# Decode attention with an MLP on one core: the first head's keys in two transfers

## The chip, the cores and the metric

The kernel runs on one core of a Trainium2 chip. A core has TensorE (matrix products, with a separate path that loads the stationary operand), VectorE, ScalarE, GpSimd, and SyncE, which here issues nearly all transfers. Sixteen DMA engines move data between the chip's memory (HBM) and the core's on-chip memory (SBUF); TensorE writes its results to accumulators (PSUM). Engines run side by side and order themselves with semaphores.

The metric is the time of one execution on the device, in microseconds. Lower is better.

## What is computed

One new token passes through an attention block with a key and value cache and then through a small MLP, each behind a layer norm and with a residual. There are 32 heads of width 128, a cache of 32768 positions, bf16 data, and a model width of 512.

```python
def _A_ref(x, k_cache, v_cache, wq, wo):
    q = (x @ wq).reshape(B, Sq, H, Dh).transpose(0, 2, 1, 3)
    scores = einsum("bhqd,bhkd->bhqk", q, k_cache) * (Dh ** -0.5)
    p = softmax(scores)
    o = einsum("bhqk,bhkd->bhqd", p, v_cache)
    return o.transpose(0, 2, 1, 3).reshape(B, Sq, H * Dh) @ wo

h = x + _A_ref(_layernorm(x), A_k_cache, A_v_cache, A_wq, A_wo)
h2 = h + _B_ref(_layernorm(h), B_w1, B_b1, B_w2)      # act = h * tanh(softplus(h))
```

K and V of one head are 8 MB each, so the caches together are 537 MB, nearly all that the kernel reads.

## The kernel before

**Tiles.** A head's K lies in SBUF as 128 partitions by 256 tiles of 128 columns (`SCOLS` = 256); the 256 tiles form two halves of `TPS` = 128. A ring of six slots holds half a K or V each: K of the even heads has slots 0 and 1, K of the odd heads slots 2 and 3, and V, for all heads, slots 4 and 5. WQ lies in slot 4 at first, WO later in a K slot.

**One head on TensorE and VectorE.** `head(i)` runs `keys(i, 0)` and `keys(i, 1)`, each 16 groups (`GPS`) of `GT` = 8 tiles. In `k_group`, TensorE transposes 8 tiles into one of four PSUM tiles (L663), VectorE copies them to `ering` (L668), and up to three groups later (`KEEP`) `scores` multiplies them with the head's query into `S_ps` (L641). `soft_max`, `soft_a`, `soft_b` and `soft_exp` then find the maximum over the partitions and form the exponentials in `pbuf`. `rest(i)` does for the head before: `soft_c` (the sum), `pv` (256 products with the tiles of V, L689) and `oev`. `turn` runs once, after head 0: it is head 0's `soft_a`, `soft_b` and `soft_exp`.

**Order.** TensorE's and VectorE's program is a loop over heads: head(0), turn, then head(i), rest(i) for the others, and at the end `mid` (the product of 31 heads with WO), the last rest, and `tail` (the rest of the projection and the MLP). On TensorE the loop body stands once and is run 32 times; the waits in it compare a semaphore with a value that is computed from the round's counter (`_loop_waits`). The addresses of the 8 key tiles of a group are also computed from the counter (`key_addresses`, L520): for each group but a head's first, that happens right after the transposes of the group before it, ahead of the scores that follow there.

**Transfers.** SyncE (SP) works through the list `order`: WQ, K0, K1, V0, K2, V1, K3, V2, and so on to WO, V31 and the MLP's weights (issues at L532). Each issue waits for what frees its place (`freed_by`): K of head h for the release of both halves of K of head h-2, V for the product of the head before with its V, and V0 for WQ's release after the projection of the query. WQ itself is issued ahead of the program's blocks (L840). A K or V is one transfer of 8 MB, other than V of the last head, which comes in six pieces after `CUTS["v"]`. For such pieces there are semaphores of their own, `cut_sems`; the heads whose V comes whole still have waits on them in the loop's body, so SP adds the missing counts once, as listed by `uncut`.

**Waits on keys.** A head's first transpose waits for "keys_in", the count of the slot pair that holds its K. Nothing waits within a head for keys.

Of the kernel before, what the change touches and what calls it, by code (L numbers as in the profile page):

```python
# [291 lines left out]
def bass_sequential_preLN__mha_block_cached__dense_activation_mish__decode_kernel(  # L292
    nc: bass.Bass,
    A_x: bass.AP,
    A_k_cache: bass.AP,
    A_v_cache: bass.AP,
    A_wq: bass.AP,
    A_wo: bass.AP,
    B_x: bass.AP,
    B_w1: bass.AP,  # L300
    B_b1: bass.AP,
    B_w2: bass.AP,
    out: bass.AP,
):
    build_kernel(nc, A_x, A_k_cache, A_v_cache, A_wq, A_wo, B_w1, B_b1, B_w2, out)


def build_kernel(nc, A_x, A_k_cache, A_v_cache, A_wq, A_wo, B_w1, B_b1, B_w2, out):
# [3 lines left out]
    H = HD // Dh  # L312
# [9 lines left out]
    TPS = 128  # L322
    SLOT = TPS * Dh
    HALVES = Sk // (128 * TPS)
    SCOLS = HALVES * TPS
    GT = 8
# [95 lines left out]

    CUTS = {"k": [], "v": [TPS // 2, TPS, 192, 224, 240]}

    def pieces(what):
        kind, h = what
        at = CUTS["v"] if what == ("v", H - 1) else []
        return list(zip([0] + at, at + [SCOLS]))  # L430

    def cut_at(kind, h, r):
        return r in [r0 for r0, _ in pieces((kind, h))]

    def uncut(what):


        kind, h = what
        for r in CUTS[kind]:
            if not cut_at(kind, h, r) and (h == 0 or cut_at(kind, h - 1, r)):  # L440
                n = 1
                while h + n < H and not cut_at(kind, h + n, r):
                    n += 1
                yield r, n
# [4 lines left out]
    order += [WO, ("v", H - 1), WL] + W1P + W2P  # L449
    cut_sems = {k: {r: sem(f"cut_{k}_{r}") for r in CUTS[k]} for k in CUTS}  # L450

# [9 lines left out]
    def slot_of(what):  # L461
        if what in HOMES:
            return HOMES[what]
        if what[0] in ("w1", "w2"):
            return HOMES[WL]
        return V_HOME if what[0] == "v" else what[1] % 2 * HALVES
# [6 lines left out]
    def ready_wait(what):  # L473
        if what == WL:
            return (s_wl, 16)
        return (ready[slot_of(what)], 16 * fills[what])

    def free_name(what):
        return "free" + "_".join(map(str, what))

    def freed_by(what):
        if what == WO:
            return done_with("k", H - 2, 0, SCOLS)
        if what[0] == "k" and what[1] > 1:
            return done_with("k", what[1] - 2, 0, SCOLS)
        if what == ("v", 0):
            return [free_name(WQ)]
        return []

    def tiles_of(what):  # L490
        return ring[:, slot_of(what):slot_of(what) + HALVES, :].rearrange("p s (r d) -> p (s r) d", d=Dh)

    def keys_of(cache, h):
        return cache[0, h, :, :].rearrange("(p r) d -> p r d", r=SCOLS)
# [8 lines left out]
    def done_with(kind, h, r0, r1):  # L503
        if kind == "v":
            return [f"pv{h}_{r1}" if r1 in V_EVENTS else f"pv{h}"]
        return [free_name(("k", h, half)) for half in range(HALVES) if r0 < (half + 1) * TPS and r1 > half * TPS]
# [1 line left out]
    events = {}  # L508

    def key_tile(S, at):  # L510
        if at == 0:
            key_addresses(S, 0)
        off = S.home + at * Dh * 2
        return ring8[:, bass.ds(off, Dh * 2)].bitcast(BF16)

    def key_addresses(S, at):

        if S.emit and S.only == PE and S.counter is not None:
            for r in range(at, at + GT):
                nc.tensor.lower_val(S.home + (r * Dh * 2 + ring_at + 2 * (Dh - 1)))  # L520

    def program(S):
# [3 lines left out]
        v = nc.vector  # L526
# [4 lines left out]
        def start(dst, src, s):  # L531
            S.dma(SP, lambda: sp.dma_start(dst, src).then_inc(s, 16))  # L532
# [3 lines left out]
        for what in order:  # L536
            slot = slot_of(what)
            if what == ("k", 1):
                S.stay(SP)
            S.wait(SP, freed_by(what))  # L540
            flat = ring[:, slot, :]
            if what[0] == "wq":
                S.wait(SP, ["b1z"])
                start(b1r[0:FJ, :], B_b1[0:FJ * 128].rearrange("(j p) -> j p", j=FJ), s_b1)
                start(b1r[FJ:FJ + 1, 0:FLAST], B_b1[FJ * 128:F].rearrange("(o p) -> o p", o=1), s_b1)
            elif what[0] == "wo":
                start(flat, A_wo.rearrange("(p j) n -> p (j n)", j=32), ready[slot])
            elif what == WL:
                start(wol_v, A_wo[(H - 1) * Dh:H * Dh, :], s_wl)
            elif what[0] == "w1":  # L550
                k = what[1]
                start(w1_v[:, k, :], B_w1[k * 128:(k + 1) * 128, :], w1_sems[k])
            elif what[0] == "w2":
                n = what[1]
                if n + 1 < len(W2_J):
                    j0, j1 = W2_J[n], W2_J[n + 1]
                    start(w2_v[:, j0:j1, :], B_w2[j0 * 128:j1 * 128, :].rearrange("(j p) n -> p j n", p=128), w2_sems[n])
                else:
                    start(w2_v[0:FLAST, FJ, :], B_w2[FJ * 128:F, :], w2_sems[n])
            else:  # L560
                kind, h = what
                rows = keys_of(A_k_cache if kind == "k" else A_v_cache, h)
                for r0, r1 in pieces(what):
                    if kind == "v" and h:
                        S.wait(SP, done_with(kind, h - 1, r0, r1))
                    start(tiles_of(what)[:, r0:r1, :], rows[:, r0:r1, :], cut_sems[kind][r0] if r0 else ready[slot])
                for r, n in uncut(what):
                    S.dma(SP, lambda r=r, n=n: sp.sem_inc(cut_sems[kind][r], 16 * n))
        S.dma(SP, lambda: sp.dma_start(out[0, 0, :].rearrange("(c m) -> c m", c=KC), outr[0:128:32, :]).then_inc(s_out, 16),
              waits=["fin"])  # L570
# [46 lines left out]
        for h in range(H):  # L617
            for kc in range(KC):
# [4 lines left out]
                       waits=(["xn0", ready_wait(("wq",))] if h == 0 and kc == 0 else ()))  # L623
# [20 lines left out]
        def flush(keep):  # L644
            while len(pend) > keep:
                scores(*pend.pop(0))

        def k_group(h, half, gi):
            what = ("k", h)
            bg = count[0]  # L650
            count[0] += 1
            tb = T_b[bg % NT]
            for r in range(GT):
                at = half * TPS + gi * GT + r
                waits = []
                if r == 0:
                    if at == 0:
                        waits.append("keys_in")
                    waits.append("identb")
                names = []  # L660
                if r == GT - 1:
                    names = [f"trb{bg}"] + ([free_name(what + (half,))] if gi == GPS - 1 else [])
                S.step(PE, lambda r=r, at=at: t_.matmul(tb[:, r * 128:(r + 1) * 128], key_tile(S, at), identb[:, :],  # L663
                                                        is_transpose=True, start=True, stop=True),
                       name=(names or None), waits=waits, kind=f"tr{bg % (2 * GPS)}")
            if half * TPS + (gi + 1) * GT < SCOLS:
                key_addresses(S, half * TPS + (gi + 1) * GT)
            S.step(DVE, lambda: v.tensor_copy(ering[:, bg % NE, :, :].rearrange("p r d -> p (r d)"), tb[:, :]),  # L668
                   name=f"ev{bg}", waits=[f"trb{bg}"],
                   kind=f"ev{bg % (2 * GPS)}")  # L670
            pend.append((h, half * TPS + gi * GT, bg))
            flush(KEEP)


        def pv(h, r0, r1):
            what = ("v", h)
            vt = tiles_of(what)
            for r in range(r0, r1):
                waits = []
                if r == 0:  # L680
                    waits += [f"exp{h}", ready_wait(what)]
                if r in CUTS["v"]:
                    waits.append((cut_sems["v"][r], 16 * (h + 1)))
# [43 lines left out]
        def keys(h, half):  # L727
            for gi in range(GPS):
                k_group(h, half, gi)
# [107 lines left out]
    log = {}  # L837
    counted = _Sched(nc, False, events, sems, log)
    program(counted)
    nc.sync.dma_start(ring[:, slot_of(WQ), :], A_wq.rearrange("(p k) n -> p (k n)", k=KC)).then_inc(ready[slot_of(WQ)], 16)  # L840
    with nc.Block() as block:
        for eng_name, attr in ((POOL, "gpsimd"), (SP, "sync"), (DVE, "vector"), (ACT, "scalar"), (PE, "tensor")):
            emitter = _Sched(nc, True, events, sems, log, only=eng_name)

            def _run(eng, emitter=emitter):
                program(emitter)
            getattr(block, attr)(_run)
            assert emitter.cnt == counted.cnt
# [31 lines left out]
```

## Time and profile before

| | us |
|---|---|
| median of 3 runs | 1288.19 (1287.94 to 1292.16) |
| profiled execution, its own time | 1288.21 |
| its span in the profile | 1286.4 |
| TensorE busy (products / loads) | 1017.4 / 989.9 |
| VectorE busy | 715.6 |
| ScalarE busy | 20.7 |

The mean granted clock of TensorE was 0.769 of full speed.

How to read it: the page gives, for one execution, the busy time of each engine, then the span in 40 slices with the busy tenths of each engine, the granted clock, the busy share of the 16 DMA engines and the GB/s. The chain of waits is followed back from the last instruction, at each step to what released it; its pieces give start, length and what ran. "issue" is time in which an engine waited for nothing that the profile shows. In the timeline a row gives the start, the length, the engine, the line and the operands, and in brackets the idle time before it with what ended it. In the view by windows a share of the DMA engines above 1 in a short window comes from packets that are counted where they begin.

### The profile page before, as it was taken

Reading aid. Unit: us, or ns where it says so; the run is one execution under the profiler, and the core shown is the slowest. Engines: PE = TensorE matmul, PEld = TensorE weight load, DVE = VectorE, ACT = ScalarE, POOL = GpSimd, SP = SyncE. Lnnn points to the kernel's source line nnn. Section 1 sums busy time; section 2 is a strip of 40 time slices with the busy share of each in tenths; the row PEclk is TensorE's granted clock in tenths of the full one; section 3 lists DMA queues with packets and bytes.
Section 4 is the critical chain, followed back from the end, with each engine's and each line's share of the span. In section 5 each row is a group of like instructions: output and inputs, shape, how many; then the busy total and the mean of one; then the engine's idle time right before and its main releaser. Section 6 shows DMA issues by size and latency. Waiting matters only on the chain.

```text
span 1286.4 us, 54403 instructions
## 1 busy us (share of the span) xinstructions
PE 1017.4 (79%) x25044; PEld 989.9 (77%) x25044; DVE 715.6 (56%) x1252; ACT 20.7 (2%) x71; POOL 0.8 (0%) x8
## 2 busy tenths in 40 slices
PE   1789777897777887777887777887777987777987
PEld 1789777887777887777887777887777887777985
DVE  0676444666545666544666454666445666444661
ACT  0000000000000000000000000000000000000000
POOL 0000000000000000000000000000000000000000
PEclk9888677887767887777887677887767887777885
DMA  9978999999999999999999999999999999999998
GB/s 422 419 336 359 424 424 454 426 424 452 428 424 434 446 424 424 454 426 424 450 430 424 424 456 424 424 454 426 424 442 438 424 424 454 426 424 452 428 423 354
DMA packets 12440, 548.35 MB, mean 426 GB/s; under 512 B 1327, under 2 KB 2832, under 8 KB 3600
## 3 DMA queue, kind: packets, MB, share of 16 engines
q1 hardware_dynamic: 12430, 548.22, 98.8%
q8 instruction: 8, 0.13, 0.0%
q10 hardware_dynamic: 2, 0.00, 0.0%
HBM read 548.21 MB, written 0.00 MB: 426 GB/s over the span
## 4 chain that ended last, share of the span: by engine, by line
DMA 55%; DVE 23%; PE 18%; SPq 2%; issue 1%; POOL 0%; POOLq 0%
DMA ring<-in_A_k_cache_dram 55%; DVE ering L668 23%; PE ops L689 9%; PE tps L663 7%; SPq L532 2%; PE sps L641 1%; PE hlp L713 1%; PE hlp L708 1%; DMA ring<-in_B_w_dram 1%; PE hlp L723 0%; PE tps L825 0%; DVE pmax L702 0%; DVE outr L830 0%; DVE gmax L710 0%; SPq L68 0%
## 5 line engine op out<-in xcount | busy, mean ns | idle before, releaser
L663 PE MATMUL tps<-identb,ring 128*128 128x128 bf16 x8192 | 668.7, 232 | 232.7 <-DMA ring<-in_A_k_cache_dram 227.3
L668 DVE COPY ering<-tps 128x1024 bf16<-128x1024 bf16 x1024 | 669.1, 692 | 283.4 <-PE tps L663 282.6
L663 PEld LDWEIGHTS tps<-identb,ring 128*128 x8192 | 522.5, 104 | 235.4 <-issue 235.4
L641 PE MATMUL sps<-qcur,ering 128*128 128x1 bf16 x8192 | 343.8, 164 | 7.7 <-DVE ering L668 6.6
L641 PEld LDWEIGHTS sps<-qcur,ering 128*128 128x128 bf16 x8192 | 309.3, 97 | 10.6 <-DVE ering L668 9.4
L689 PEld LDWEIGHTS ops<-pbuf,ring 128*128 128x128 bf16 x8192 | 226.6, 103 | 15.6 <-issue 12.3
L689 PE MATMUL ops<-pbuf,ring 128*128 128x1 bf16 x8192 | 231.2, 165 | 2.4 <-DMA ring<-in_A_v_cache_dram 2.4
L697 DVE TENSOR_TENSOR oT<-ops,rtotc 128x1 f32 x31 | 5.0, 161 | 107.1 <-PE ops L689 107.1
L710 DVE TENSOR_REDUCE gmax<-hlp 1x1 f32<-1x128 f32 x32 | 8.9, 279 | 63.1 <-PE hlp L708 63.1
L715 DVE TENSOR_SCALAR nbias<-hlp 128x1 f32<-128x1 f32 x32 | 5.1, 159 | 63.5 <-PE hlp L713 63.5
L718 ACT ACTIVATE pbuf<-sps,nbias 128x256 bf16<-128x256 f32 x32 | 15.2, 474 | 1236.4 <-PE ops L689 1171.5
L702 DVE TENSOR_REDUCE pmax<-sps 128x1 f32<-128x256 f32 x32 | 13.6, 425 | 14.3 <-PE sps L641 14.3
L708 PE MATMUL hlp<-ident,pmax 128*1 128x128 f32 x64 | 17.7, 375 | 2.4 <-issue 2.4
L713 PE MATMUL hlp<-gmax,onesmat 1*128 1x1 f32 x64 | 18.5, 356 | 0.4 <-DVE gmax L710 0.4
L713 PEld LDWEIGHTS hlp<-gmax,onesmat 1*128 1x128 f32 x64 | 15.8, 304 | 1.3 <-DVE gmax L710 0.9
L723 PE MATMUL hlp<-esum,onesmat 128*128 128x1 f32 x64 | 12.3, 261 | 5.0 <-issue 1.8
L723 PEld LDWEIGHTS hlp<-esum,onesmat 128*128 128x128 f32 x64 | 9.8, 192 | 7.6 <-issue 7.6
L620 PE MATMUL hlp<-xnT,ring 128*128 128x1 bf16 x128 | 3.5, 165 | 9.1 <-DMA ring<-in_A_wq_dram 9.1
L620 PEld LDWEIGHTS hlp<-xnT,ring 128*128 128x128 bf16 x128 | 3.5, 104 | 9.2 <-issue 9.2
L725 DVE RECIPROCAL rtotc<-hlp 128x1 f32<-128x1 f32 x32 | 5.4, 168 | 3.9 <-PE hlp L723 2.4
L624 DVE CAST qT<-hlp 128x32 bf16<-128x32 f32 x1 | 0.2, 192 | 11.3 <-PE hlp L620 11.3
L718 ACT ACTIVATION_READ_ACCUMULATOR pbuf<-sps,nbias 128x1 f32 x32 | 6.1, 192 | 0.0
(75 smaller groups left out, 37.8 us busy)
## 6 DMA issues: line engine op xcount, KB each, us to landing
ring<-in_A_v_cache_dram SPq DMA_DIRECT2D x3, 2048.0 KB, 11.2
ring<-in_A_wq_dram SPq DMA_DIRECT2D x1, 4096.0 KB, 12.1
ring<-in_A_wo_dram SPq DMA_DIRECT2D x1, 4096.0 KB, 35.2
ring<-in_B_w_dram SPq DMA_DIRECT2D x4, 344.0 KB, 16.6
ring<-in_A_v_cache_dram SPq DMA_DIRECT2D x1, 1024.0 KB, 14.2
ring<-in_A_v_cache_dram SPq DMA_DIRECT2D x2, 512.0 KB, 15.4
ring<-in_B_w_dram SPq DMA_DIRECT2D x1, 640.0 KB, 16.3
ring<-in_A_k_cache_dram SPq DMA_DIRECT2D x32, 45.1
```

The lines of the kernel that those rows point to most:

```text
L532: S.dma(SP, lambda: sp.dma_start(dst, src).then_inc(s, 16))
L620: S.step(PE, lambda h=h, kc=kc: t_.matmul(Q_REG[:, h:h + 1], wq_v[:, kc, h * Dh:(h + 1) * Dh], xnT[:, 0, kc:kc + 1], start=(kc == 0), stop ...
L641: S.step(PE, lambda r=r: t_.matmul(S_ps[:, col0 + r:col0 + r + 1], ering[:, bg % NE, r, :], qcur[:, :], start=True, stop=True), name=(name ...
L663: S.step(PE, lambda r=r, at=at: t_.matmul(tb[:, r * 128:(r + 1) * 128], key_tile(S, at), identb[:, :], is_transpose=True, start=True, stop ...
L668: S.step(DVE, lambda: v.tensor_copy(ering[:, bg % NE, :, :].rearrange("p r d -> p (r d)"), tb[:, :]), name=f"ev{bg}", waits=[f"trb{bg}"], ...
L689: S.step(PE, lambda r=r: t_.matmul(o_ps[:, 0:1], vt[:, r, :], pbuf[:, r:r + 1], start=(r == 0), stop=(r == SCOLS - 1)), name=(names or Non ...
L702: S.step(DVE, lambda: v.tensor_reduce(pmax[:, :], S_ps[:, 0:SCOLS], AXX, ALU.max), name=f"pmax{h}", waits=[f"qkh{h}"], kind="pmax")
L708: S.step(PE, lambda: t_.matmul(A_REG, pmax[:, :], ident[:, :], start=True, stop=True), name=f"A{h}", waits=[f"pmax{h}", "ident", f"rcp{h - ...
L710: S.step(DVE, lambda: v.tensor_reduce(gmax[:, :], A_REG, AXX, ALU.max), name=f"gmax{h}", waits=[f"A{h}"], kind="gmax")
L713: S.step(PE, lambda: t_.matmul(B_REG, onesm[0:1, :], gmax[:, :], start=True, stop=True), name=f"B{h}", waits=[f"gmax{h}", "consts0"], kind ...
L718: S.step(ACT, lambda: a.activation(pbuf[:, :], S_ps[:, 0:SCOLS], ACTF.Exp, bias=nb[:, :], scale=SC, accum_out=esum[:, :]), name=f"exp{h}", ...
L723: S.step(PE, lambda: t_.matmul(C_REG, onesm[:, :], esum[:, :], start=True, stop=True), name=f"C{h}", waits=[f"exp{h}"], kind="C")
```

## The change

Three things change.

- K of head 0 is issued as two transfers, tiles 0 to 127 and tiles 128 to 255. The first counts on the slot's semaphore as before, the second on a new one, `cut_sems["k"][128]`.
- In the loop body, the transpose of tile 128 (group 16, the first of the second half) has a wait of its own on that semaphore, for 16 more with each head. The addresses of group 16 are no longer computed behind the transposes of group 15, ahead of the scores there, but behind these scores, just before the transposes of group 16. With the wait comes one register instruction on TensorE for the value it waits for. The body is one instruction longer.
- For the 31 heads whose K still comes whole, SP adds 16 x 31 to the new semaphore, once, right after the issue of K2.

```diff
-    CUTS = {"k": [], "v": [TPS // 2, TPS, 192, 224, 240]}
+    CUTS = {"k": [TPS], "v": [TPS // 2, TPS, 192, 224, 240]}
 
     def pieces(what):
         kind, h = what
-        at = CUTS["v"] if what == ("v", H - 1) else []
+        at = CUTS[kind] if what in (("k", 0), ("v", H - 1)) else []
         return list(zip([0] + at, at + [SCOLS]))
...
     def key_tile(S, at):
-        if at == 0:
-            key_addresses(S, 0)
+        if at in [0] + CUTS["k"]:
+            key_addresses(S, at)
...
-                for r, n in uncut(what):
+
+                for r, n in uncut(what) if kind == "v" else [(r, H - 1) for r in CUTS["k"] if h == 2]:
                     S.dma(SP, lambda r=r, n=n: sp.sem_inc(cut_sems[kind][r], 16 * n))
...
                     waits.append("identb")
+                if at in CUTS["k"]:
+                    waits.append((cut_sems["k"][at], 16 * (h + 1)))
...
-            if half * TPS + (gi + 1) * GT < SCOLS:
-                key_addresses(S, half * TPS + (gi + 1) * GT)
+            after = half * TPS + (gi + 1) * GT
+            if after < SCOLS and after not in CUTS["k"]:
+                key_addresses(S, after)
```

## The prediction

> **What bounds the kernel now.** I read the page first, for the engine that is busy throughout and for the stretches where it is not.
>
> ```profile
> span 1286.4 us, 54403 instructions
> ...
> DMA  9978999999999999999999999999999999999998
> GB/s 422 419 336 359 424 424 454 426 424 452 428 424 434 446 424 424 454 426 424 450 430 424 424 456 424 424 454 426 424 442 438 424 424 454 426 424 452 428 423 354
> ...
> q1 hardware_dynamic: 12430, 548.22, 98.8%
> q8 instruction: 8, 0.13, 0.0%
> ...
> DMA 55%; DVE 23%; PE 18%; SPq 2%; issue 1%; POOL 0%; POOLq 0%
> ```
>
> The transfers fill 98.8% of the span. So the kernel is bound by its 548 MB, except where the queue runs dry: slices 3 and 4 (64 to 129 us) move 336 and 359 GB/s where later ones move 424 or more. The view by windows confirms it (columns: window and length, busy time and count of each engine, granted clock, DMA share, GB/s).
>
> ```profile
> 64.00:104.00 40.00, 34.98 (x829) 33.50 (x827) 24.17 (x45) 1.13 (x4) 0.00 (x0) 0.76 0.70 296
> 90.00:91.00 1.00, 1.00 (x31) 1.00 (x29) 1.00 (x3) 0.00 (x0) 0.00 (x0) 1.00 0.00 0
> 178.00:1183.00 1005.00, 809.65 (x20124) 791.37 (x20124) 575.57 (x988) 14.70 (x52) 0.00 (x0) 0.76 1.00 434
> ```
>
> From 64 to 104 us the engines are busy 0.70 of the time; afterwards the share is 1.00. Why, is seen in the chain of waits (start, length, what) and in the timeline of the first 180 us (SPq rows are issues).
>
> ```profile
> 1.96 31.54 DMA ring<-in_A_k_cache_dram
> 44.61 1.54 issue
> 48.90 0.88 PE tps L663 x8
> 49.97 0.53 PE tps L663 x8
> 50.67 0.47 PE tps L663 x8
> 51.32 0.47 PE tps L663 x8
> 52.52 1.06 issue
> 58.64 2.12 issue
> 66.07 1.96 issue
> 69.56 0.80 issue
> 70.37 3.60 PE tps L663 x32
> 73.99 18.82 DVE ering L668 x29
> 93.75 1.66 PE ops L689 x64
> 98.23 3.52 PE ops L689 x128
> 102.21 40.68 DMA ring<-in_A_k_cache_dram
> 142.89 0.33 issue
> 175.60 45.07 DMA ring<-in_A_k_cache_dram
> 1181.35 45.65 DMA ring<-in_A_k_cache_dram
> 1276.03 7.41 DMA ring<-in_B_w_dram
> ```
>
> ```profile
> 12.98 3.55 PE L620 MATMUL hlp<-xnT,ring 128*128 128x1 bf16 x128 [9.10 <-DMA ring<-in_A_wq_dram]
> 16.56 0.33 SPq L532 DMA_DIRECT2D ring<-in_A_v_cache_dram  x1
> 33.91 2.31 PE L663 MATMUL tps<-identb,ring 128*128 128x128 bf16 x20 [17.38 <-DMA ring<-in_A_k_cache_dram]
> 64.53 0.33 SPq L532 DMA_DIRECT2D ring<-in_A_k_cache_dram  x1
> 101.77 0.33 SPq L532 DMA_DIRECT2D ring<-in_A_v_cache_dram  x1
> 134.49 0.33 SPq L532 DMA_DIRECT2D ring<-in_A_v_cache_dram  x1
> ```
>
> Between the key issues at 175.60 and 1181.35 lie 26 heads, 1005.75 / 26 = 38.68 us each, so one 8 MB half of a head (K or V) takes 19.34 us. K0 lands at 1.96 + 31.54 = 33.50; K1, V0 and K2 follow without a break and end at 33.50 + 3 x 19.34 = 91.5. The next transfer, V1, shares its slots with V0 and waits until head 0's product with V is over, 98.23 + 3.52 = 101.75. K3 lands at 102.21 + 40.68 = 142.89; less two transfers, 104.2. The queue therefore loses 104.2 - 91.5 = 12.7 us here, and what puts V1 so late is a pure compute chain that starts when K0 has landed: head 0 (33.91), its softmax, head 1 (70.37), the product (93.75 to 101.75). TensorE idled 17.38 us ahead of it.
>
> Later there is no such loss: a K issued at 175.60 lands after 45.07 us, though it and the V ahead of it need 38.68, so V was issued some 6.4 us before the queue ran dry.
>
> **The change, part by part.** *K0 in two pieces.* WQ has landed by 12.98 and the whole K0 was usable at 33.91, 20.93 us for 8 MB, 1.59 us more than 19.34. No row says in which half the 1.59 falls. If in the second, the first half is usable at 12.98 + 9.67 = 22.65; if in the first, at 12.98 + 20.93 - 9.67 = 24.24. I take 24.0, near the late end, which promises less. TensorE is ready long before, 12.98 + 3.55 = 16.5. Head 0 starts 33.91 - 24.0 = 9.9 us sooner.
>
> The extra issue on SP is 0.33 us at about 2 us, behind WQ's 12 us of transfer; the issues behind it (K1, then V0 after the wait for WQ's release at 16.56) find a queue with work until 33 us. Cost nothing; uncovered, 0.33.
>
> *The second half's wait, head 0.* The 17th group, the first of the second half, starts at 48.90 now, 15.0 us after the first. Shifted, it wants its keys at 39.0, and they land at about 33.5, as the whole does now. TensorE does not stop; cover, 5.5 us.
>
> *Does the rest of head 0 shift rigidly?* It holds three stalls of "issue" (1.54, 1.06, 2.12) and slow groups: from 48.90 to 49.97 a group takes 1.07 us, from 50.67 to 51.32 0.65. The same instructions in the same order, again after an idle of many us, so I take the same length. Bounds, from the first transpose to the release of the keys (33.91 to K2's issue at 64.53, 30.6 us now): with all 32 groups at 1.07 and the 4.7 us of stalls 38.9, 8.3 lost; with the 22.4 us that head 1 takes from 70.37 to 73.99 + 18.82 = 92.81, 8.2 won. Between them I allow a stretch like that of head 1's start, 12 slow groups more, 12 x 0.42 = 5.0 us lost, and the ceiling of 12.7 on the other side.
>
> *The wait in TensorE's loop, the register addition for its value, and the two address computations that now follow it.* One instruction more per head, 32 in all, and behind it stand the transposes of group 16 and all that follows. No row has this wait. The nearest is 142.89: 0.33 us from a key's landing to the first transpose, which contains a wait and two such address computations. So 0 to 0.33 per head; no gain is possible, since nothing is taken out. In heads 0 and 1, on the chain, I charge 0.15 each, 0.3 in all, as VectorE paces the groups there (29 in 18.82 us, 0.65 each) and has several tiles to work on. For the later heads the view of waits has a row (us in total, times, longest):
>
> ```profile
> PE tps L663 <- DMA ring<-in_A_k_cache_dram: 227.3, 30, 17.4
> ```
>
> Without the first, 17.4, that is 209.9 / 29 = 7.2 us a head in which TensorE stands idle for keys, so 0.33 is hidden; uncovered it would be 30 x 0.33 = 9.9 us.
>
> *SP's count for the whole heads.* It stands behind the K2 issue, which waits for head 0's release: 64.53 now, about 55 then. Head 1 wants it for its 17th group, which VectorE copies at 73.99 + 13 x 0.65 = 82.4 now; TensorE runs up to three groups ahead, so 80 now and 70 then. 15 us of cover. What queues behind it on SP is V1, not wanted there before 92.
>
> *What is late next.* With V1 issued at 101.77 - 9.6 = 92.2, the queue still runs dry for 12.7 - 9.6 = 3.1 us, so the gain is the whole shift. K1 (52.8), V0 (72.2) and K2 (91.5) have all landed before their users at 60.8, 84.2 and 92.2 (70.37, 93.75 and 101.75, each less 9.6). From V1 on every issue and landing moves with it: V2's issue (134.49, 8.4 us before K3's end at 142.89) moves too, and the end, at 1276.03 + 7.41 a landing of the last weights, is transfer-bound as before.
>
> The sum: 9.9 - 0.3 = 9.6 us. The profiled execution took 1288.21 us (span 1286.4 and 1.81 around it), the median of the runs 1288.19. 1288.21 - 9.6 = 1278.6.
>
> [...]
>
> **The rivals.** *No gain: the transfers set the time, and the earlier start ends in another wait.* For it: 98.8%, and 55% of the chain is DMA. It needs a wait between K0 and V1's issue that does not move. Each landing above comes before its user, the tightest K2 by 0.7 us. Against it, too: the 12.7 us are idle time of the very resource that binds. Time 1288.2. Chance 0.04.
>
> *The change does not do what it says: the first half isn't usable sooner.* If the engines serve both halves of K0 side by side, the first lands with the second at about 33.5, and TensorE starts at 33.9. For it: both are queued within a microsecond. Against it: WQ was queued just ahead of K0 and landed by 12.98, with K0 20.9 us later, so pieces come in order. Time 1288.5, with the 0.3 of the waits. Chance 0.03.
>
> *Slower: the longer loop body is fetched anew in every round.* Place: TensorE's loop, one instruction longer. Now the queue for instructions moves 8 packets in the whole span, so the loop is loaded once; the stalls of the first pass (1.54, 1.06, 2.12, 1.96, 0.80, together 7.48 us) show what loading costs. If the body no longer fitted, each round would lose 7.48, and from 6.4 us on it decides, as V is then issued after the queue has run dry: 1.1 us a head, 30 heads, 33 us, less 9.6 gained: 1288.2 + 23 = 1312. Against it: one instruction among over a thousand. Chance 0.04, and 0.02 for others on that side.
>
> [...] The trace's 8 packets in 32 rounds show that it is not refetched now.
>
> *More than forecast: head 0 runs shorter too and the hole closes.* 12.7 us, 1275.5; inside the range.
>
> **How the numbers follow.** Forecast and its variants 0.87, no gain 0.04, not sooner 0.03, slower 0.06. What a measurement of this kernel can tell from no change is about 0.3%, 3.9 us. The range runs from the closed hole, 1275.5, to 5.0 us lost on slow groups, 1278.6 + 5.0 = 1283.6; past it lie the rivals and the longest head 0 (8.3 lost, 1286.9), together under 0.2. The last leaves too little to be told, so of the 0.87 I give 0.02 to no change: faster 0.85, same 0.09, slower 0.06.
>
> **What would show each step.** Right: the first transposes at 23 to 24.3 us; no idle of TensorE on keys at the middle of head 0; K2's issue near 55 and V1's near 92; the share of the queue from 64 to 104 us near 0.9; keys every 38.7 us after that; 8 packets of instructions. Wrong: the first transpose at 34 (not sooner), V1 at 102 (the chain did not move), a wait before the 17th group from head 1 on (the count is late), or stalls of "issue" in later rounds, with more instruction packets.

## The result, and the profile after

The changed kernel takes 1281.96 us (median of 5 runs, 1281.40 to 1282.46); the kernel before takes 1288.65 us (median of 5, 1287.94 to 1292.16). The ratio is 0.9942, with a 95% interval of 0.9928 to 0.9957: faster by 0.58%, 6.7 us where 9.6 were forecast. The change does what it says and the gain comes from where it was expected; 2.9 us of it are missing, and the experiments are about these.

The page after, in the lines shown of before:

```profile
span 1279.6 us, 54437 instructions
...
DMA  9979999999999999999999999999999999999998
GB/s 425 420 339 426 445 440 426 426 426 459 426 426 426 449 436 426 426 426 459 426 426 426 453 432 426 426 434 451 426 426 426 457 428 426 426 436 449 426 426 355
...
q1 hardware_dynamic: 12574, 548.22, 99.3%
q8 instruction: 8, 0.13, 0.0%
```

The fourth slice moves 426 GB/s where it moved 359; the third, 339, is as poor as before. Instructions are 34 more (32 register instructions, one transfer, one count), and their queue still moves 8 packets: the loop is not fetched anew. The same windows:

```profile
64.00:104.00 40.00, 38.12 (x903) 37.33 (x901) 28.05 (x47) 0.57 (x2) 0.00 (x0) 0.80 0.83 350
90.00:91.00 1.00, 1.00 (x24) 0.97 (x21) 0.00 (x0) 0.00 (x0) 0.00 (x0) 0.50 0.00 0
178.00:1183.00 1005.00, 811.23 (x20114) 793.94 (x20112) 575.16 (x988) 14.73 (x52) 0.00 (x0) 0.76 1.00 433
```

The share of the DMA engines from 64 to 104 us rose from 0.70 to 0.83, not to the 0.9 expected: the hole is smaller and not closed. In the bulk nothing changed (1.00, 433 GB/s). The timeline after, first transposes and issues of K2, V1 and V2:

```profile
24.30 3.59 PE L666 MATMUL tps<-identb,ring 128*128 128x128 bf16 x32 [7.75 <-DMA ring<-in_A_k_cache_dram]
...
56.28 0.33 SPq L532 DMA_DIRECT2D ring<-in_A_k_cache_dram  x1
...
95.31 0.33 SPq L532 DMA_DIRECT2D ring<-in_A_v_cache_dram  x1
...
127.90 0.33 SPq L532 DMA_DIRECT2D ring<-in_A_v_cache_dram  x1
```

Against the rows of before: the first transpose is 33.91 - 24.30 = 9.6 us sooner, K2's issue 64.53 - 56.28 = 8.3, V1's 101.77 - 95.31 = 6.5, V2's 134.49 - 127.90 = 6.6. The start is right within 0.3; what was gained there is lost between the first transpose and V1's issue. The chain of waits after shows where:

```profile
34.57 2.25 issue
...
41.86 4.62 issue
46.47 0.27 PE sps L642 x4
46.74 0.88 PE tps L666 x8
47.62 0.19 PE sps L642 x8
47.81 0.88 PE tps L666 x8
...
57.80 3.06 issue
...
62.39 0.79 issue
63.19 3.55 PE tps L666 x32
...
91.51 0.59 issue
92.10 3.19 PE ops L693 x114
...
95.75 40.67 DMA ring<-in_A_k_cache_dram
```

Before, there were 1.54 + 1.06 + 2.12 + 1.96 + 0.80 = 7.48 us of "issue" up to V1's issue; now 2.25 + 4.62 + 3.06 + 0.79 + 0.59 = 11.31. That is 3.8 us more, all in the first pass through the loop. The 0.80 and 0.79 among them stand ahead of head 1's first transposes and don't belong to the first pass alone: ahead of head 2's, too, there is such a gap, of 0.88 us before and 0.87 after. The row of before:

```profile
102.61 3.59 PE L663 MATMUL tps<-identb,ring 128*128 128x128 bf16 x32 [0.88 <-issue]
```

Without them the stalls of the first pass are 6.68 us before and 10.52 after. Each sum is that of one profiled execution.

The packet records of the trace say what these waits are. The queue for instructions has one packet of 16 KB at each of these times (us from the span's start), and its eighth near the end, at 1284.8 before and 1277.9 after:

```
before  19.5  43.8  51.2  58.3  65.5  72.7  94.7
after   19.5  34.3  43.9  51.1  58.2  65.4  89.6
```

TensorE's long stalls end 2.3 to 2.6 us after such a packet has begun (after: 36.82, 46.47, 60.85, 92.10). In all kernels measured the stalls of head 0 fall at the same places of the program, behind the 4th transpose of the 14th group, behind 4 scores that follow the 21st group's transposes, and behind the 5th transpose of the 29th group, though not each kernel has all three. In the trace of before 694, 950 and 1206 instructions of TensorE lie ahead of these places, 256 from one to the next; in that of after 694 and 950 lie ahead of the first two. From this I read the stalls so: the loop is fetched block by block while TensorE runs through it for the first time, 256 instructions in a packet of 16 KB, and TensorE stands when the next block is late. The packets of the middle stand 7.1 to 9.6 us apart, where a block without stalls or slow groups takes 4.9 us (from 29.5 on the chain of after does a group every 0.65 us; a group has 34 instructions, 16 loads, 16 products and 2 for addresses, so 256 are 7.5 groups).

### The profile page after: what moved, and what is told of

Same layout as the page of the kernel before. It is cut to its first block, busy times and chain, and to the rows that moved or that the text cites. A ratio compares the mean times of both kernels' runs of the same rounds, so it can differ in the third digit from the quotient of the medians.

```text
span 1279.6 us, 54437 instructions
## 1 busy us (share of the span) xinstructions
PE 1019.0 (80%) x25044; PEld 992.2 (78%) x25044; DVE 716.1 (56%) x1252; ACT 20.8 (2%) x71; POOL 0.8 (0%) x8
## 4 chain that ended last, share of the span: by engine, by line
DMA 55%; DVE 23%; PE 18%; SPq 2%; issue 2%; POOL 0%; POOLq 0%
DMA ring<-in_A_k_cache_dram 54%; DVE ering L672 23%; PE ops L693 9%; PE tps L666 7%; SPq L532 2%; PE sps L642 1%; PE hlp L717 1%; PE hlp L712 1%; DMA ring<-in_B_w_dram 1%; PE hlp L727 0%; PE tps L829 0%; DVE pmax L706 0%; DVE outr L834 0%; DVE gmax L714 0%; SPq L68 0%
```

## The experiments

Each is set against runs of the kernel before on the same chip.

**The wait alone.** The changed loop, with K0 whole.

```diff
-        at = CUTS[kind] if what in (("k", 0), ("v", H - 1)) else []
+        at = CUTS[kind] if what in (("v", H - 1),) else []
...
-    ... else [(r, H - 1) for r in CUTS["k"] if h == 2]:
+    ... else [(r, H) for r in CUTS["k"] if h == 0]:
```

> The loop body of the changed kernel (wait at tile 128, register instruction, moved address computations), but K0 whole, as before; SP counts for all 32 heads. Of the 9.6 us forecast 2.9 are missing, and three theories say where. Fetch theory: head 0's first pass through the loop is held up by instruction fetches that queue behind data packets, and these stalls grew from 7.5 to 11.3 us; the wait itself costs nothing, so this kernel takes the time of before, 1288.2 to 1289, with stalls of about 7.5 us again. Wait theory: the wait costs 2 to 3 us on the chain of heads 0 and 1, so 1290.5 to 1291.5. Clock theory (TensorE's slow stretches fall otherwise when it starts sooner): as before, 1288.2 to 1289.

Measured: 1288.66 us (11 runs) beside 1289.05, ratio 0.9996 (0.9987 to 1.0005). The wait, its register instruction and the moved address computations cost nothing that can be measured. The stalls up to head 1 come to 2.19 + 1.23 + 1.85 + 2.28 + 0.80 = 8.4 us, 0.9 more than in the kernel before with its 7.48: so much two traces of nearly the same program can differ, and the 3.8 us of the change are well beyond that. The wait theory falls.

**K1 in halves.**

```diff
-        at = CUTS[kind] if what in (("k", 0), ("v", H - 1)) else []
+        at = CUTS[kind] if what in (("k", 0), ("k", 1), ("v", H - 1)) else []
...
+                if what == ("k", 2):
+                    S.wait(SP, [(s_k1, 16)])
```

The second half of K1 counts on a semaphore of its own, `s_k1`.

> The changed kernel, with K1 too as two transfers of 128 tiles (SP waits for the second after it has issued K2, before it adds the counts). TensorE's program is the same; a partition's run in K1 is 32 KB instead of 64, so a packet holds its DMA engine half as long. Fetch theory: the fetches after 35 us wait behind packets of K1, now half as long; the gap from the fetch at 34.9 to the next falls from 9.6 to about 5 us, the stall of 4.62 us to under 1.5, head 0 ends 3 to 4 us sooner, V1 is issued at 91 to 92.5 instead of 95.3, and the time is 1278 to 1279.5. Clock theory and wait theory: the size of K1's packets changes nothing, V1 at about 95.3, time 1281.5 to 1282.5.

Measured: 1281.88 us, ratio 0.9939 (0.9926 to 0.9953), the time of the changed kernel. K1's packets did get half as long: one of 64 KB takes 2.42 us in the changed kernel (median, 35 to 50 us), one of 32 KB 1.21 us here. K2's issue, at 52.68, comes 3.6 us sooner than after, V1's no sooner:

```profile
52.68 0.33 SPq L533 DMA_DIRECT2D ring<-in_A_k_cache_dram  x1
95.78 0.33 SPq L533 DMA_DIRECT2D ring<-in_A_v_cache_dram  x1
```

The chain of this kernel:

```profile
35.41 0.17 issue
...
40.61 2.42 issue
...
49.48 0.75 issue
...
54.20 4.22 issue
...
59.95 0.80 issue
...
89.21 3.36 issue
```

Head 0 did get shorter, as the fetch theory said (from 2.25 + 4.62 to 0.17 + 2.42 + 0.75 us of stalls). But the stall that follows head 0, at the start of its softmax and now beside V0's packets, grew from 3.06 to 4.22, and a stall in the product of head 0 from 0.59 to 3.36. The gap between the second fetch of the list above, at 34.3 us (34.9 in the expectation, which counts packets from 0.6 us earlier), and the next fell from 9.6 to 7.5 us, not to 5. So my expectation for the time was wrong, and with it the simple form of the theory, that a fetch waits for a fixed number of packets and so half as long behind half as long ones. The time and V1 are those that the clock theory gave; what tells the two theories apart is the kernel with K1 held back, below.

**K1 in halves, K0 whole.** The same as above, with `("k", 0)` left out of the cut kernels' list and SP adding 16 for head 0 right after K0's issue.

> K0 whole, K1 as two transfers, with the loop body of the changed kernel. No key arrives sooner. Fetch theory: head 0's stalls of 1.54, 1.06 and 2.12 us fall to under 1.5 together, as its fetches meet shorter packets, so V1 is issued 3 to 4 us sooner than 101.8 and the time is 1284.5 to 1285.5. Clock and wait theories: 1288.2 to 1289 (or 1291 with the price of the wait).

Measured: 1288.60 us, ratio 0.9997 (0.9987 to 1.0006); V1 at 102.31. The stalls of head 0 are 0.94 + 1.60 + 2.84 us, no less than before. A miss for the fetch theory in that simple form: shorter packets of K1 alone bring nothing.

**K1 in halves and V0 in six pieces.**

```diff
-        at = CUTS[kind] if what in (("k", 0), ("k", 1), ("v", H - 1)) else []
+        at = CUTS[kind] if what in (("k", 0), ("k", 1), ("v", 0), ("v", H - 1)) else []
```

> As the kernel with K1 in halves, and V0 in six pieces like the last V (16, 16, 16, 8, 4 and 4 KB a partition). Fetch theory: the fetch after head 0 meets V0's packets; its stall of 3.06 us falls under 1.5, V1 is issued at 89 to 91, before K2 has landed at about 92, and the queue no longer runs dry: share of the DMA engines from 64 to 104 us at 0.98 or more, time 1276 to 1278.5. Clock and wait theories: 1281.5 to 1282.5.

Measured: 1279.67 us, ratio 0.9925 (0.9911 to 0.9939), 2.3 us better than the changed kernel, short of the 1276 to 1278.5 expected. V1 is issued at 93.36 (89 to 91 expected), the share from 64 to 104 us is 0.92 (0.98 expected), and the stall that follows head 0 is still 2.99 us where under 1.5 was expected. What the smaller pieces change is little and uneven.

**K1 held back.** If the stalls come from data in the queue, they must vanish when the queue is empty. This kernel issues K1 only when head 0's keys are released.

```diff
     def freed_by(what):
...
+        if what == ("k", 1):
+            return done_with("k", 0, 0, SCOLS)
```

> The changed kernel, with K1 issued only when head 0's keys are released, so that from about 33.5 us on no data packet stands beside head 0's instruction fetches. So far: the wait alone costs nothing, and halving K1's packets let head 0 end 3.6 us sooner but moved neither V1's issue nor the time, since later fetches stalled for longer. Fetch theory: with the queue empty the stalls of head 0 after 37 us (4.62 us at 41.9) fall to under 0.5, and the keys are released (K1's issue) at 47 to 50 us instead of 56.3. Clock theory: the stalls of issue stay as they are, release at 55 us or later. Either way the queue stands idle for about 15 us, so the time is 1290 to 1294 by the first, 1297 or more by the second.

Measured: 1292.61 us (8 runs), ratio 1.0030 (1.0020 to 1.0041). Its chain of waits, from the first key to K1's issue and at the product of head 0:

```profile
24.43 3.23 PE tps L668 x32
...
33.91 0.06 issue
33.97 0.38 PE tps L668 x4
...
45.57 0.48 PE tps L668 x8
...
46.13 22.89 DMA ring<-in_A_k_cache_dram
...
98.21 3.00 issue
```

From 24.43 to K1's issue at 46.13 it does the same 32 groups without a stall longer than 0.06 us: 21.7 us, where the changed kernel needs 56.28 - 24.30 = 32.0. The instruction packets of this stretch begin at 31.7, 35.6, 40.5 and 45.5, the last three 5 us apart, close to the 4.9 us in which a block is used up. At 98 us, with K2 on its way, a stall of 3.00 us is back. The view by windows puts the two kernels side by side, first the changed one, at the same stretch (clock, share and GB/s are the last three columns):

```profile
29.50:46.50 17.00, 10.13 (x248) 9.88 (x245) 10.63 (x17) 0.00 (x0) 0.00 (x0) 0.99 1.06 455
46.50:53.50 7.00, 7.00 (x111) 7.00 (x112) 3.98 (x6) 0.00 (x0) 0.00 (x0) 0.54 0.97 414
```

and K1 held back:

```profile
29.50:46.50 17.00, 16.94 (x426) 16.77 (x423) 16.82 (x27) 0.00 (x0) 0.00 (x0) 1.00 0.12 46
```

With 455 GB/s beside it TensorE does 248 products in 17 us, with 46 GB/s 426, at the same granted clock of 0.99 to 1.00. That settles that the stalls come from the data in flight, not from the clock. The changed kernel then loses more: after the 4.62 us stall its clock stands at 0.54 from 46.5 to 53.5 us, and a group takes 1.07 us (the chain of after, 46.74 to 47.81). The release, 46.1 us, is a little ahead of the 47 to 50 expected; the time lies in the first bracket, the price of a queue that is idle from about 33.5 to 46 us.

**K0 in quarters.**

```diff
-    CUTS = {"k": [TPS], "v": [TPS // 2, TPS, 192, 224, 240]}
+    CUTS = {"k": [TPS // 2, TPS, 192], "v": [TPS // 2, TPS, 192, 224, 240]}
```

> The changed kernel with K0 in four transfers of 64 tiles (and waits at tiles 64 and 192 too). The first keys arrive some 5 us sooner, at about 19 us. Rigid theory, that of the prediction: head 0 and all behind it move by 5 us until the hole closes: V1's issue at 90 to 91, time 1277 to 1278.5. Fetch theory: TensorE starts 5 us sooner and gives 2 us or more of it back in longer stalls; V1 at 92 to 94, time 1279 to 1281.5.

Measured: 1276.84 us (4 runs), ratio 0.9903 (0.9888 to 0.9918), 5.1 us better than the changed kernel. Its chain and then its window:

```profile
18.07 0.42 issue
18.49 3.60 PE tps L666 x32
...
33.98 3.26 issue
...
43.65 2.75 issue
...
51.22 4.88 issue
...
57.63 0.88 issue
...
86.50 0.80 issue
...
90.95 41.09 DMA ring<-in_A_k_cache_dram
```

```profile
64.00:104.00 40.00, 36.57 (x888) 35.79 (x886) 26.72 (x46) 0.56 (x2) 0.00 (x0) 0.79 0.95 403
```

TensorE starts 24.30 - 18.49 = 5.8 us sooner, and V1 is issued at 90.51, 4.8 us sooner. The stalls, 12.6 us where 11.31 stood, grew by 1.3. V1 lies in the rigid theory's bracket and the time 0.2 us below it. So this step moved nearly rigidly, as the prediction's view has it, and the fetch theory's 2 us or more were not given back: a miss on that side. How long a fetch waits is not the same from one kernel to the next.

**Quarters, K1 in halves, V0 in pieces.** Cuts as in the two kernels above.

> K0 in four transfers, K1 in two, V0 in six. Fetch theory: head 0 starts at about 19 us, V1 is issued at 90 to 92, about when K2 lands, and the hole is nearly closed: time 1277.5 to 1279.5. Rigid theory: V1 at 88 to 89, hole closed, 1275.5 to 1277.

Measured: 1276.79 us, ratio 0.9905 (0.9890 to 0.9920).

```profile
64.00:104.00 40.00, 32.22 (x786) 31.43 (x783) 22.43 (x40) 0.56 (x2) 0.00 (x0) 0.74 1.02 437
```

V1 is issued at 88.50, and the share from 64 to 104 us is that of the bulk: the hole is closed. V1 and the time lie in the rigid theory's brackets. The time is no better than with quarters alone, and 1.3 us over the 1275.5 that the prediction worked out for a closed hole. Quarters alone had left little: its K3 lands at 90.95 + 41.09 = 132.04, here at 131.19, and 0.85 us is less than the 1.1 to 1.6 us by which the four runs of each kernel differ among themselves.

**K2 in halves too.** The kernel with K1 in halves and V0 in pieces, K2 cut like K1, with a semaphore that SP waits for behind K3's issue.

> K0, K1 and K2 in halves, V0 in six pieces. The kernel without K2's halves stalled 1.69 us at 88.5 on the fetch of the product's code, which queued behind 64 KB packets of K2. Fetch theory, if the length of a packet matters: that stall falls under 1 us, V1 is issued at 92 to 93, time 1278.5 to 1279.7. If it doesn't (the fetches stay 7 us apart whatever the packets, as seen with K1 in halves): V1 at 93 to 95 and 1279.5 to 1281.

Measured: 1278.86 us, ratio 0.9927 (0.9913 to 0.9940); V1 at 92.07, the stall 1.44 us instead of 1.69. V1 and the time lie in the first bracket; the stall, expected under 1 us, does not. At this size the runs don't tell the two apart.

## Why the prediction came out as it did

**What bounds the kernel: right.** The loss was the idle queue between K2 and V1, behind a compute chain that starts at K0's landing. Moving the start moved V1, V2 and the end: 6.5, 6.6 and 6.7 us. With the hole closed (quarters and pieces) the share goes to 1.02 and the further earliness brought nothing (1276.79 us beside 1276.84).

**The start, 9.9 us sooner: right.** Measured 9.6. The first half is usable at 24.30, near the late end of the bounds 22.65 to 24.24, and just outside. That the shift comes to the 9.6 us of the sum is luck: the start was 0.3 short, and the 0.3 charged for the waits did not show up.

**Wait and count: right.** No wait on keys in the middle of head 0: the chain after goes through the 17th group without one. Head 1's 29 copies take 18.81 us where they took 18.82, so the count was not late there. Price of the loop's wait 0.3 us charged, nothing measurable with the wait alone (ratio 0.9996).

**Head 0 shifts rigidly: the step that failed in size.** The prediction said of head 0 "the same instructions in the same order, again after an idle of many us, so I take the same length", and took its three stalls and the two behind it along unchanged. All but the last of these, the 0.80 us, are waits for instructions in the first pass, and their length depends on the data in flight: 6.7 us before, 10.5 after, and in head 0 none over 0.06 with the queue empty. Of the 9.6 us, head 0 up to its release gave back 1.4 (stalls 2.2 more, fewer slow groups against that), the stall at its softmax 1.1 and head 1 with the product 0.7. The bounds held this (5.0 lost on slow groups was allowed, 3.1 were lost), though for another reason than the one named.

**The rivals.** No gain and not sooner: refuted by the start at 24.30 and the ratio. Refetch in every round: refuted by the 8 packets. The price that it put on one loading does show: 6.7 to 11.7 us of stalls in the first pass, in the nine kernels with data in flight beside head 0.

**What stays open.** Why a fetch waits as long as it does. That data in flight delay it shows at the product of head 0 as well: where the queue was idle there (before, the wait alone, K1 in halves with K0 whole) the packet with its code begins 1.0 to 1.1 us after the product's start, in the seven kernels with K2 still on its way 3.1 to 5.7 us after it. But the wait is not proportional to the length of the packets beside it: in the kernel with K1 in halves, beside packets of 1.21 us in place of 2.42, the fetches still stand 7.1 to 8.1 us apart. A kernel with its code loaded ahead of the data was not tried.

The best version found is K0 in quarters, the change with two more cuts: 1276.84 us, 0.97% faster than before and 5.1 us faster than the change.

## What to carry to other kernels

A queue that is busy 98.8% of the span can still be worth feeding (here 6.7 us with one cut, 11.7 with three): look for the one stretch where its share drops and follow back what issued the next transfer late; a landing that starts that chain can be cut into pieces. When a chain of compute is moved, don't take its stalls along as fixed lengths: those of the first pass through the loop depended here on what was in the DMA queue at that moment (6.7 us before, 10.5 after the move), so give them bounds of their own. And stop cutting when the stretch shows the share of the bulk: here the cuts that brought it from 0.95 to 1.02 gained nothing.

## What the runs showed of the hardware

- The first pass through TensorE's loop cost 6.7 us of stalls before, 10.5 in the changed kernel (data at 455 and 414 GB/s from 29.5 to 53.5 us) and 11.7 with K0 in quarters. With the queue empty (46 GB/s), the 32 groups of head 0 had no stall over 0.06 us.
- Slow groups followed some of the stalls: after 4.62 us without work (the changed kernel, from 41.86) the granted clock was 0.54 for 7 us (0.99 ahead of it), and a group took 1.07 instead of 0.65 us. The length of the stall alone did not decide that: behind one of only 1.54 us (before, from 44.61) the clock was 0.53, behind one of 2.42 us (K1 in halves and V0 in pieces, from 40.46) it stayed at 1.00. What decides it was not shown. The windows behind these two, first that of before, with the clock in the third column from the end:

```profile
46.80:50.20 3.40, 3.40 (x54) 3.40 (x53) 2.23 (x4) 0.00 (x0) 0.00 (x0) 0.53 0.80 347
42.90:48.00 5.10, 5.06 (x121) 4.89 (x121) 4.36 (x7) 0.00 (x0) 0.00 (x0) 1.00 0.97 414
```

- Filling the hole in the queue took a shelter away: before, the fetch at 94.7 us met an idle queue and the product of head 0 ran without a stall; in the seven kernels with K2 still on its way there it stood for 0.59 us (the change) to 3.36 us (K1 in halves).
